# Moving four PSUM casts from VectorE to ScalarE, and the bank of TensorE's filler matmuls

## The chip, the cores and the metric

The kernel runs on 1 core of a Trainium2 chip. The metric is the device time of one execution in microseconds (us). In what follows PE is TensorE (matmuls), ACT is ScalarE, DVE is VectorE, POOL is GpSimd and SP is SyncE, as in the profile; PSUM is the accumulator memory that TensorE writes, here 8 banks of 512 fp32 columns, and only ScalarE and VectorE read it in this kernel.

## The reference

A sigmoid attention over 8 batches of 12 heads, 448 positions and 64 features, followed by a gated MLP over the 3584 tokens:

```python
scores = (q @ k.T) / sqrt(64) - log(448)      # per batch and head, 448 x 448
x = sigmoid(scores) @ v                       # the attention output
x = x.transpose(0, 2, 1, 3).reshape(3584, 768)
h = x @ w_in                                  # 768 -> 2048
g = h * sigmoid(beta * h)
out = g @ w_out                               # 2048 -> 768
```

## The kernel before, in words

All matmuls take fp16 operands and accumulate in fp32. The work is cut into tasks, each of a few instructions of one engine. The 96 (batch, head) pairs form 24 **groups** of four heads; a group g has two "slots", 2g and 2g+1, of two heads each, and a batch has three groups. For each group:

- `sG.j` (`visit`, L229) or, for the first batch, `hG.half.k` (`half_visit`, L249): the scores of a block of keys, by matmuls of 32 rows (L969, several at a time in parts of the array) into pairs of PSUM banks, one pair for each slot or tile.
- `eG.j.i` (`weigh`, L222 and L978): ScalarE reads such a pair and writes sigmoid(scale * score + bias) to SBUF as fp16 (L979). One instruction reads 896 columns; a few read 448.
- `aG.half.i` (`attend`, L279): the product with v, matmuls of L991, one bank for each slot.
- `xS.half` (L308): the bank is cast to fp16 into `xT` by `put_x` (L1000), 448 columns for each slot, or 224 in the first batch, where the queries are taken in two halves.

The MLP's first product of a batch (`d`, and `p`, an arrangement with fewer multiplications) runs on `xT`, with a sigmoid on ScalarE (L1024) and a product on VectorE (L1033); the second product (`tP.i.part`, L1009 and L1011) takes two tiles of 128 tokens at a time, in seven products, and its `o` tasks copy and add banks into `osb` (L1152 is the copy on ScalarE, `oP.1`).

**The order.** TensorE's order of tasks and the order of the loads on POOL's queue are written out by hand (`PE_ORDER`, L768, and `LOAD_ORDER`, L804). The function `plan` (L614) goes through them with estimated durations, when the program is built, and fixes from that the banks, the buffers and the order of the tasks on ScalarE and VectorE: each of these takes the ready task that has been ready longest. The order that the plan gives is emitted with a manual schedule; on the chip each engine runs its instructions strictly in that order, and semaphores make it wait for what it needs. The waits are set for each bank: an instruction that writes a bank waits for whoever read the bank before.

**Fillers.** Between 5 and 36 us of the plan, where TensorE is planned to wait, `plan` puts matmuls of zeros there (L740): `fills` (L595) gives them a free bank if there is one, and otherwise writes only the unused 64 columns (448 to 511) of the bank of the first filler task (`work.idle_bank`), which is bank 0. They are emitted by `idle` (L871, matmul in L873), right before the task that waits.

**The places that the change touches.** In the plan of the kernel before the following are met:

- TensorE's order has `h1.1.1`, then 18 filler matmuls of 64 columns in bank 0, then `a0.1.0`, then four fillers in bank 7, then `h2.1.1`. The task `h1.1.0` ahead of them wrote the bank pairs (6, 7) and (0, 1), which ScalarE's `eh1.1.0.0` and `eh1.1.0.1` read in this order; `h1.1.1` wrote the pairs (2, 3) and (4, 5), which `eh1.1.1.0` and `eh1.1.1.1` read. `a0.1.0` writes bank 6, and `h2.1.1` writes the pairs (0, 1) and (6, 7).
- For groups 6 and 7 (both of batch 2) TensorE's order has `a6.0.0`, `s7.0`, then products of tile pair 1, with `s8.0` after eight of them; and `a7.0.0`, `s8.2`, three products of tile pair 2, `s8.3`. `s8.1`, `s8.2` and `s8.3` all use the bank pairs (0, 1) and (6, 7), in this order. `s8.3` has 16 matmuls in two passes: the first four of a pass write the pair (0, 1), the next four (6, 7). The casts of group 6 are `x12` and `x13`, those of group 7 are `x14` and `x15`. ScalarE's order is `e7.1.1`, `e7.0.0`, `e7.0.1`, `o1.1` and later `e8.1.1`, `e8.2.0`, `e8.2.1`, `o2.1`, `e8.3.0`.

Of the kernel before, what the change touches and what calls it, by code (L numbers as in the profile page):

```python
# [15 lines left out]
B, H, S, D = 8, 12, 448, 64  # L16
# [9 lines left out]
NPAIR = H // 2  # L26
# [9 lines left out]
QH = S // 2  # L36
# [13 lines left out]
def mm(n):  # L50
    return max(n / 2400 + 0.0025, 0.057)
# [4 lines left out]
WARM = 36.0  # L56
SHORT = 0.03
START_END, START_RATE = 7.3, 115.0
# [16 lines left out]
def dve_us(n):  # L75
    return 0.076 + 1.04e-3 * n, 0.24 + 1.04e-3 * n
# [15 lines left out]

WHOLE = tuple(range(16))
SPLIT = (6, 7)
ENGINES = ("PE", "ACT", "DVE", "POOL", "SP", "Z")
FREE_AT = {"PE": 1.0, "ACT": 3.3, "DVE": 0.9, "POOL": 1.2, "SP": 0.7, "Z": 0.0}
MODES = {"s": 0, "s64": 1, "v": 2, "v64": 3, "d": 4}
# [13 lines left out]
class Work:  # L111
# [167 lines left out]
    def attend(self, g, c0=0, n=S, parts=((0, 1),)):  # L279
        k, b = self.k, g // QPB  # L280
        for part in parts:
            slots = [2 * g + x for x in part]
            ats = {(s, jt): self.at[s, jt, c0] for s in slots for jt in range(JF + 1)}
            us = JF * len(slots) * mm(n) + SWITCH + mm(n)
            first = b not in self.x_first
            name = f"a{g}.{c0 // QH}.{part[0]}"
            if c0 == 0 and n == QH and part == (0,):
                vs = self.v_low[b]
            else:
                vs = self.v_ready[b]  # L290
            pe = self.pe_task(name, us, [w for w, _ in ats.values()] + vs, mode="v", end_mode="v64", take=["xT"] if first else [], banks="S" * len(slots), good=n == S)
            if first:
                self.x_first[b] = pe
            for w in {id(w): w for w, _ in ats.values()}.values():
                self.users.setdefault(w.i, [w, 0])
            order = [(s, i, jt) for i, s in enumerate(slots) for jt in range(JF)] + [(s, i, JF) for i, s in enumerate(slots)]
            pe.emit = lambda t, order=order, ats=ats: k.values(
                [(s, t.bank[i], jt, ats[s, jt][0].slot["attn"], ats[s, jt][1]) for s, i, jt in order], self.v_first[b].slot["v"], n
            )
            for w in {id(w): w for w, _ in ats.values()}.values():  # L300
                last = self.last_user.get(w.i)
                if last is not None:
                    last.give.remove((w, "attn"))
                    pe.after.append(last)
                pe.give.append((w, "attn"))
                self.last_user[w.i] = pe
            for i, s in enumerate(slots):
                c = self.add("DVE", f"x{s}.{c0 // QH}", dve_us(n), [pe], give_banks=[(pe, i)])  # L308
                c.emit = lambda t, i=i, s=s, pe=pe: k.put_x(self.x_first[b].slot["xT"], s % NPAIR, c0, n, pe.bank[i])
                self.x_ready[b, c0].append(c)  # L310
                self.x_by[b, s % NPAIR, c0] = c
            self.av[g, c0, part[-1]] = pe
        if c0 + n == S:
            if g % QPB == QPB - 1:
                pe.give.append((self.v_first[b], "v"))
# [204 lines left out]
    def build(self):  # L520
# [39 lines left out]
        for c0 in (0, QH):  # L560
            for dc in range(NDC):
                if dc not in WHOLE:
                    firsts.append(self.plain(0, dc, c0, QH))
                elif c0:
                    firsts += self.split(dc) if dc in SPLIT else [self.plain(0, dc, 0, S)]
        free = self.add("Z", "xfree0", (0.0, 0.02), firsts, give=[(self.x_first[0], "xT")])
# [28 lines left out]
def fills(us, banks, first):  # L595

    if us < 0.12:
        return None
    if not banks:
        return [(first[0], S, FREE_COLS, int(us / SHORT))]  # L600
    long = int(us / mm(512))
    short = int((us - long * mm(512)) / mm(128))
    return [(banks[0], 0, n, c) for n, c in ((512, long), (128, short)) if c]
# [10 lines left out]
def plan(work, pe_names, load_names):  # L614
# [6 lines left out]
    bank_free, bank_busy, good = [0.0] * 8, [False] * 8, [False] * 8  # L621
    users = [[] for _ in work.tasks]
    left = [len(t.deps) for t in work.tasks]
    ready_at = [0.0] * len(work.tasks)
    ready = {e: [] for e in ENGINES}
    split_columns(queue["PE"])
# [6 lines left out]
    free, events, n = dict(FREE_AT), [], 0  # L633
    pe_end = FREE_AT["PE"]
# [41 lines left out]
    def can(t):  # L676
        return all(slot(r) is not None for r in t.take) and (not t.banks or find(t.banks) is not None)

    def begin(t, now):
        for r in t.take:  # L680
            i = t.slot[r] = slot(r)
            busy[r][i] = True
        extra = 0.0
        if t.banks:
            got, mend = find(t.banks)
            for x in got:
                bank_busy[x] = True
                good[x] = t.good
            t.bank = got[::2] if t.banks[0] == "D" else got
            t.mend = mend if t.banks[0] == "F" else []  # L690
            extra = 0.19 if any(t.mend) else 0.0
        t.start = now
        order.append(t)
        return extra

    now = 0.0
    while events:
        now = events[0][0]
        batch = []
        while events and events[0][0] <= now + 1e-9:  # L700
            batch.append(heapq.heappop(events))
        for _, kind, _, x in batch:
            if kind:
                for u in users[x.i]:
                    left[u.i] -= 1
                    if left[u.i] == 0:
                        ready_at[u.i] = now
                        ready[u.eng].append(u)
                for t, r in x.give:
                    i = t.slot[r]  # L710
                    busy[r][i], slots[r][i] = False, now
                for t, i in x.give_banks:
                    for y in (t.bank[i], t.bank[i] + 1) if t.banks[0] == "D" else (t.bank[i],):
                        bank_busy[y], bank_free[y] = False, now
        for e in ENGINES:
            if free[e] > now + 1e-9:
                continue
            if e in queue:
                if at[e] >= len(queue[e]):
                    continue  # L720
                t = queue[e][at[e]]
                if left[t.i] or not can(t):
                    continue
                if e == "POOL":
                    if at[e] >= 8 and lands[at[e] - 8] > now:
                        heapq.heappush(events, (lands[at[e] - 8], 0, n, e))
                        n += 1
                        continue
                    begin(t, now)
                    at[e] += 1  # L730
                    free[e] = now + t.occ
                    kb, rate = t.kb
                    dma_free = service(max(dma_free, now + 1.83), kb, rate)
                    late = 4.3 if now > 55 else 2.7 if now > 12 else 0.3 if dma_free < 6.3 else 1.2 if dma_free < 11 else 1.8
                    lands.append(dma_free + min(late, 2.0))
                    done = dma_free + late
                else:
                    wait = now - pe_end
                    rest = [x for x in range(8) if not bank_busy[x] and bank_free[x] <= pe_end]
                    t.fill = fills((wait - 0.15) / (2 if now < START_END else 1), rest, work.idle_bank.bank) if 5 < now < WARM else None  # L740
                    extra = begin(t, now)
                    at[e] += 1
                    if mode is not None and t.form != mode:
                        extra += SWITCH
                    mode = t.form if t.mode == "d" else t.end_mode
                    pe_end = free[e] = now + extra + t.occ
                    done = now + extra + t.lat
            else:
                cand = [t for t in ready[e] if can(t)]
                if not cand:  # L750
                    continue
                t = min(cand, key=lambda t: (ready_at[t.i] - t.soon, t.i))
                ready[e].remove(t)
                begin(t, now)
                free[e] = now + t.occ
                done = now + t.lat
                if t.kb:
                    dma_free = max(dma_free, now + 1.0) + t.kb[0] / t.kb[1]
            heapq.heappush(events, (free[e], 0, n, e))
            t.done = done  # L760
            heapq.heappush(events, (done, 1, n + 1, t))
            n += 2
# [51 lines left out]
class Emitter:  # L814
# [182 lines left out]
                    tile_position=(base, hh * D),  # L997
                )

    def put_x(self, x, p, c0, n, bank):  # L1000
        self.nc.vector.tensor_copy(out=self.xT[x][:, p, c0 : c0 + n], in_=self.bank(bank, n))  # L1001

# [234 lines left out]
```

## Time and profile before

| what | value |
|---|---|
| time, median of 3 runs | 372.1 us (371.88 to 372.85) |
| time of the profiled execution | 372.93 us |
| its span (first to last instruction) | 370.6 us |
| PE busy | 364.2 us, 98% of the span |
| DVE busy | 278.1 us, 75% |
| ACT busy | 250.5 us, 68% |
| data moved by DMA | 34.81 MB |

The profiled execution is one run under the hardware profiler. Its own time is 2.3 us longer than its span, the time around the instructions. In a row of the timeline stand the start, the duration, engine, line, operation, output and input with the shapes, the count of instructions merged into the row, and in brackets how long the engine had been idle and whom it waited for. Matmuls overlap: the profiler's end of one lies a little after the start of the next.

### The profile page before, as it was taken

The page shows a single profiled execution, that of the slowest core. Times are in us where ns is not written, and L with a number is a line of the kernel's source. Part 1 is how long each engine was busy: PE and PEld are TensorE (multiplying, and loading weights), DVE is VectorE, ACT ScalarE, POOL GpSimd, SP SyncE. Part 2 cuts the span into 40 slices and gives each one's busy share as a digit, 9 for nine tenths or more (in the row PEclk, how much of TensorE's full clock was granted, in tenths as well). Part 3 has the DMA queues.
Part 4 walks back from the last instruction along what each step waited for, and adds up shares of the span by engine and source line. Part 5 has one row for each costly group of instructions (what it writes and reads, how often), then busy time and mean ns, then how long its engine had stood idle before and what let it go on. Part 6 is the DMA issues. An engine that isn't in the chain of part 4 may idle for free.

```text
span 370.6 us, 10079 instructions
## 1 busy us (share of the span) xinstructions
PE 364.2 (98%) x4182; PEld 229.2 (62%) x4182; DVE 278.1 (75%) x577; ACT 250.5 (68%) x407; POOL 67.0 (18%) x113
## 2 busy tenths in 40 slices
PE   8989999999999999999999999999999999999996
PEld 4644445744556954479544794489544894579664
DVE  3436889999666988678787698689686686777865
ACT  5879975676467776768777689778756787546400
POOL 7837143500006301040004300070000000000000
PEclk9999999999999999999999999999999999999999
DMA  8999999932137942593016930095021300120124
GB/s 164 194 201 195 204 204 201 200 41 54 33 88 96 231 58 38 123 135 83 3 27 126 202 68 0 3 153 109 0 56 33 88 2 3 33 55 0 45 84 128
DMA packets 42845, 34.81 MB, mean 94 GB/s; under 512 B 21920, under 2 KB 39344, under 8 KB 42800
## 3 DMA queue, kind: packets, MB, share of 16 engines
q0 software_dynamic: 36688, 22.47, 43.6%
q1 hardware_dynamic: 5968, 11.65, 11.4%
q8 instruction: 32, 0.52, 0.6%
q14 instruction: 13, 0.11, 0.1%
q10 hardware_dynamic: 144, 0.07, 0.1%
HBM read 45.62 MB, written 11.01 MB: 153 GB/s over the span
## 4 chain that ended last, share of the span: by engine, by line
PE 92%; DVE 4%; DMA 2%; ACT 1%; issue 1%; POOL 0%; POOLq 0%
PE ps L1011 49%; PE ps L1009 20%; PE ps L969 11%; PE ps L991 10%; DMA raw<-in_k_dram 2%; DVE gt L1033 2%; PE ps L873 2%; DVE ps L1033 1%; DVE kT L956 1%; ACT sg L1024 0%; ACT attn L979 0%; POOL raw L893 0%; DVE xT L1001 0%; ACT ps L1088 0%; DVE sum L1033 0%
## 5 line engine op out<-in xcount | busy, mean ns | idle before, releaser
L979 ACT ACTIVATE attn<-ps 128x896 f16<-128x896 f32 (+1 forms) x171 | 145.1, 904 | 56.0 <-PE ps L969 55.2
L1024 ACT ACTIVATE sg<-ps,beta_sb 128x448 f32<-128x448 f32 x128 | 76.4, 637 | 29.1 <-PE ps L1011 16.4
L1033 DVE TENSOR_TENSOR gt<-ps,sg 128x448 f16<-128x448 f32 x128 | 75.2, 614 | 7.2 <-ACT sg L1024 6.6
L1009 PEld LDWEIGHTS <-w_in 128*64 128x64 f16 x1308 | 64.2, 110 | 6.1 <-issue 1.8
L1011 PEld LDWEIGHTS <-sum 128*128 128x128 f16 x480 | 44.8, 98 | 35.1 <-issue 8.1
L1033 DVE TENSOR_TENSOR sum<-gt 128x1024 f16<-128x1024 f16 x70 | 46.8, 683 | 22.7 <-PE ps L1011 21.1
L1011 PEld LDWEIGHTS <-w_in 128*128 128x128 f16 x531 | 50.5, 98 | 17.7 <-issue 2.9
L1011 PE MATMUL ps<-xT,w_in 128*128 128x224 f16 (+1 forms) x327 | 54.1, 304 | 0.0
L969 PE MATMUL ps<-qT,kT 32*128 32x448 f16 (+3 forms) x864 | 50.7, 340 | 0.1
L1009 PE MATMUL ps<-xT,w_in 128*64 128x224 f16 (+1 forms) x636 | 48.5, 277 | 0.0
L1001 DVE CAST xT<-ps 128x448 f16<-128x448 f32 (+1 forms) x54 | 29.0, 566 | 25.0 <-PE ps L991 24.9
L1011 PE MATMUL ps<-w_T,sum 128*128 128x384 f16 (+1 forms) x256 | 45.7, 322 | 0.0
L1033 DVE TENSOR_TENSOR ps<-ps,S 128x224 f32<-128x224 f32 x90 | 34.2, 392 | 14.9 <-ACT ps L1088 7.4
L1009 PE MATMUL ps<-xs,w_in 128*64 128x224 f16 x672 | 45.0, 259 | 0.1
L991 PE MATMUL ps<-attn,v 128*64 128x448 f16 (+3 forms) x432 | 42.0, 338 | 0.0
L1033 DVE TENSOR_TENSOR osb<-ps,osb 128x384 f32<-128x384 f32 (+1 forms) x72 | 38.6, 542 | 4.4 <-PE ps L1011 2.3
L1011 PE MATMUL ps<-w_out,sum 128*128 128x384 f16 x224 | 40.9, 327 | 0.0
L1011 PE MATMUL ps<-w_out,gt 128*128 128x384 f16 x212 | 39.6, 327 | 0.3 <-DVE xT L1001 0.3
L913 POOL DMA_DIRECT2D v<-in_v_dram x32 | 20.1, 631 | 104.8 <-PE ps L991 88.7
L991 PEld LDWEIGHTS <-v 128*64 128x64 f16 (+1 forms) x432 | 20.7, 108 | 20.0 <-issue 11.9
L1011 PEld LDWEIGHTS <-gt 128*128 128x128 f16 x212 | 19.1, 98 | 19.0 <-issue 8.0
L969 PEld LDWEIGHTS <-kT 32*128 32x128 f16 (+1 forms) x864 | 13.4, 96 | 24.1 <-issue 22.6
(38 smaller groups left out, 242.0 us busy)
## 6 DMA issues: line engine op xcount, KB each, us to landing
out_dram<-osb SPq DMA_DIRECT2D x100, 96.0 KB, 1.9
raw<-in_k_dram POOLq DMA_DIRECT2D x23, 224.0 KB, 7.2
raw<-in_q_dram POOLq DMA_DIRECT2D x21, 224.0 KB, 7.1
v<-in_v_dram POOLq DMA_DIRECT2D x32, 144.0 KB, 6.4
w_in<-in_moe_w_in_dram POOLq DMA_DIRECT2D x8, 384.0 KB, 9.3
w_out<-in_moe_w_out_dram POOLq DMA_DIRECT2D x4, 768.0 KB, 14.2
v<-in_v_dram POOLq DMA_DIRECT2D x16, 48.0 KB, 6.4
out_dram<-osb SPq DMA_DIRECT2D x4, 192.0 KB, 2.1
```

The lines of the kernel that those rows point to most:

```text
L873: self.nc.tensor.matmul(self.ps[:, x, c0 : c0 + n], self.still[:, 0:P], self.still[:, 0:n], start=(c0 == 0), stop=True, skip_group_check=True,
L913: self.nc.gpsimd.dma_start(out=to, in_=rows[:, :, JF * i * D : JF * (i + 1) * D])
L956: self.nc.vector.transpose(out=to, in_=frm)
L969: self.nc.tensor.matmul(self.ps[base : base + nk, d + hh, u0 : u0 + n], self.kT[k][lo : lo + BLK, jt * P : jt * P + nk, e], self.qT[q][lo ...
L979: self.nc.scalar.activation(out=self.at[slot][:, :, 0:n], in_=self.ps[:, d : d + 2, 0:n], func=AF.Sigmoid, bias=NEG_LOG_S, scale=MSCALE,)
L991: self.nc.tensor.matmul(self.bank(x, n)[hh * D : (hh + 1) * D], self.vs[v][base : base + nk, 2 * (s % NPAIR) + hh, jt], self.at[at][base : ...
L1001: self.nc.vector.tensor_copy(out=self.xT[x][:, p, c0 : c0 + n], in_=self.bank(bank, n))
L1009: self.nc.tensor.matmul(out[lo : lo + D], w[:, lo : lo + D], x, tile_position=(0, lo), **kw)
L1011: self.nc.tensor.matmul(out, w, x, **kw)
L1024: self.nc.scalar.activation(out=self.sg[slot][:, 0:n], in_=self.bank(x, n), func=AF.Sigmoid, bias=0.0, scale=self.beta_sb[:, dc : dc + 1],)
L1033: self.nc.vector.tensor_tensor(out=out, in0=in0, in1=in1, op=getattr(ALU, op))
```

## The change

Three things change in the text of the program. A new constant `XA` names the groups 6 and 7; for these `attend` gives the four casts `x12` to `x15` to ScalarE, with `put_x` using ScalarE's copy, instead of VectorE. And `plan` keeps a set `read` of the banks that a planned reader is reading at the time, so that fillers without a free bank go to a bank outside this set whose reader has not begun.

```diff
+XA = (6, 7)
...
             for i, s in enumerate(slots):
-                c = self.add("DVE", f"x{s}.{c0 // QH}", dve_us(n), [pe], give_banks=[(pe, i)])
-                c.emit = lambda t, i=i, s=s, pe=pe: k.put_x(self.x_first[b].slot["xT"], s % NPAIR, c0, n, pe.bank[i])
+                on_act = g in XA
+                c = self.add("ACT" if on_act else "DVE", f"x{s}.{c0 // QH}", (copy_us if on_act else dve_us)(n), [pe], give_banks=[(pe, i)])
+                c.emit = lambda t, i=i, s=s, pe=pe: k.put_x(self.x_first[b].slot["xT"], s % NPAIR, c0, n, pe.bank[i], on_act)
...
+    read = set()
+
     def begin(t, now):
...
+        for o, i in t.give_banks:
+            read.update((o.bank[i], o.bank[i] + (o.banks[0] == "D")))
...
                 for t, i in x.give_banks:
+                    read -= {t.bank[i], t.bank[i] + (t.banks[0] == "D")}
...
-                    t.fill = fills((wait - 0.15) / (2 if now < START_END else 1), rest, work.idle_bank.bank) if 5 < now < WARM else None
+                    beside = [x for x in work.idle_bank.bank + list(range(7, -1, -1)) if x not in read and (bank_busy[x] or bank_free[x] <= pe_end)]
+                    t.fill = fills((wait - 0.15) / (2 if now < START_END else 1), rest, beside or work.idle_bank.bank) if 5 < now < WARM else None
...
-    def put_x(self, x, p, c0, n, bank):
-        self.nc.vector.tensor_copy(out=self.xT[x][:, p, c0 : c0 + n], in_=self.bank(bank, n))
+    def put_x(self, x, p, c0, n, bank, on_act):
+        copy = self.nc.scalar.copy if on_act else self.nc.vector.tensor_copy
+        copy(out=self.xT[x][:, p, c0 : c0 + n], in_=self.bank(bank, n))
```

In the program that comes out, nothing else moves. TensorE runs the same matmuls in the same order, with the same banks but for one run of fillers: the 18 ahead of `a0.1.0` now write columns 448 to 511 of bank 5 instead of bank 0. The first of them no longer has a wait; `a0.1.0`'s first matmul and `h2.1.1`'s first matmul, which had none, now each have a wait for ScalarE, and so has `eh1.1.1.1`, which reads bank 5, for the fillers. Three other runs of 64-column fillers that stood in bank 0 stay there. On ScalarE `x12` and `x13` stand between `e7.1.1` and `e7.0.0`, and `x14` and `x15` between `e8.1.1` and `e8.2.0`; VectorE's order is the old one without these four. The queues of POOL and SP, all loads and all stores are the same.

## The prediction

> **What bounds the kernel now.** I read the page first: its busy shares, and the chain of work that ended last by engine.
>
> ```profile
> span 370.6 us, 10079 instructions
> PE 364.2 (98%) x4182; PEld 229.2 (62%) x4182; DVE 278.1 (75%) x577; ACT 250.5 (68%) x407; POOL 67.0 (18%) x113
> PE 92%; DVE 4%; DMA 2%; ACT 1%; issue 1%; POOL 0%; POOLq 0%
> ```
>
> PE is busy for 364.2 of 370.6 us and makes up 92% of the chain. So a microsecond counts only where PE stands still, or is made to. Next come the waits of PE over the whole span (us in total, times, longest).
>
> ```profile
> PE ps L873 <- ACT attn L979: 1.4, 1, 1.4
> PE ps L873 <- DVE dummy L866: 1.2, 1, 1.2
> PE ps L1011 <- DVE xT L1001: 0.3, 1, 0.3
> PE ps L873 <- issue: 0.2, 1, 0.2
> ```
>
> PE's waits come to 3.1 us. The second is the start of the kernel. The largest is a filler (L873) that waits for a weighing of ScalarE (L979): matmuls that do no work hold up TensorE. The timeline of PE shows where, that of ACT whom it waits for, and the chain of waits the last piece.
>
> ```profile
> 19.73 1.10 PE L969 MATMUL ps<-qT,kT 32*128 32x224 f16 x32
> 22.18 0.69 PE L873 MATMUL ps<-sum 128*128 128x64 f16 x18 [1.35 <-ACT attn L979]
> 22.79 0.69 PE L991 MATMUL ps<-attn,v 128*64 128x224 f16 x8
> 23.41 0.72 PE L873 MATMUL ps<-sum 128*128 128x512 f16 x4
> 24.06 0.70 PE L969 MATMUL ps<-qT,kT 32*128 32x224 f16 x16
> ...
> 20.40 0.92 ACT L979 ACTIVATE attn<-ps 128x896 f16<-128x896 f32 x1 [0.36 <-PE ps L969]
> 20.40 2.97 ACT L979 ACTIVATE attn<-ps 128x896 f16<-128x896 f32 x4 [0.36 <-PE ps L969]
> 24.82 0.92 ACT L979 ACTIVATE attn<-ps 128x896 f16<-128x896 f32 x1 [1.45 <-PE ps L969]
> ...
> 21.21 0.92 ACT attn L979
> 22.13 0.04 issue
> 22.18 0.69 PE ps L873 x18
> ```
>
> The first row is `h1.1.0` and `h1.1.1`, over at 20.83 (19.73 + 1.10). The 18 fillers should fill the wait after it. Instead the first of them waits until 22.13, the end of the second of ScalarE's four weighings: `eh1.1.0.1`, which reads banks 0 and 1. The fillers write bank 0. `a0.1.0`, at 22.79, writes bank 6, and bank 6 is read by the first weighing, over at 21.32 (20.40 + 0.92). So `a0.1.0` runs 1.47 us after its bank is free, behind a wait that isn't its own and the 0.61 us of the fillers (22.79 - 22.18).
>
> **The change, part one: the fillers in bank 5.** Bank 5 belongs to `eh1.1.1.1`, the fourth weighing; it doesn't begin before 22.8, while 18 fillers that start after `h1.1.1` are long over. So the fillers begin at once. Matmuls overlap by 0.07 (22.18 + 0.69 = 22.87, and the next row begins at 22.79), so they begin at about 20.76 and leave PE free at 20.76 + 0.61 = 21.37. `a0.1.0` also needs the first weighing: 21.32, and 0.05 for the semaphore (22.13 to 22.18). That gives 21.37 too. I take 21.38 for the start of `a0.1.0`, against 22.79: **1.41 us earlier**. Bounds: 1.47 if the wait costs nothing, and 0.61 if `a0.1.0` had to wait for the second weighing itself.
>
> What is late next? `h2.1.1` follows after `a0.1.0` and four fillers, at 24.06 - 1.41 = 22.65. Its banks 0 and 1 are free at 22.13; bank 6 needs the cast of `a0.1.0`, which moves with it. Its output goes to ScalarE, which begins at 24.82 today after 1.45 us of idleness, so ScalarE can take it up to 1.45 us earlier: 1.41 fits, by 0.04. The two are this close because ScalarE's four weighings do not move.
>
> Then the loads: the DMA queues are full in this stretch, and their data won't land earlier. The nearest load is k of group 3, transposed by VectorE after the cast of `a0.1.0`.
>
> ```profile
> 23.59 0.39 DVE L1001 CAST xT<-ps 128x224 f16<-128x224 f32 x1 [3.96 <-PE ps L991]
> 23.90 0.57 DVE L956 STREAM_TRANSPOSE kT<-raw 128x384 f32<-128x384 f32 x1
> ...
> 13.28 0.57 POOL L893 DMA_DIRECT2D raw<-in_k_dram  x1
> raw<-in_k_dram POOLq DMA_DIRECT2D x1, 224.0 KB, 8.7
> ...
> DVE xT L1001 <- PE ps L991: 8.4, 8, 4.0
> DVE gt L1033 <- ACT sg L1024: 3.5, 3, 1.8
> ...
> POOL v L913 <- PE ps L991: 88.7, 4, 40.9
> ```
>
> It is issued at 13.28 and lands 8.7 later, at 21.98; the transpose moves from 23.90 to 22.49 and still finds it. The next two rows are all the waits of VectorE between 22.5 and 76 us: none is for a DMA. So the loads have slack everywhere there. Later POOL's queue itself waits for buffers, most of all for PE, as the last row shows for the whole span; such loads move with PE. After 22.18 PE waits once more, for 0.3 us, on a cast of its own product; that moves along. So I carry the 1.41 us to the end.
>
> **Part two: the casts of group 7.** The copy on ScalarE is bounded by its own rows; the last three are a copy, a copy and a weighing in direct sequence.
>
> ```profile
> L1152 ACT COPY osb<-ps 128x384 f32<-128x384 f32 x14 | 6.8, 484 | 17.3 <-PE ps L1011 17.3
> L907 ACT CAST raw<-osb 128x448 f16<-128x448 f32 x1 | 0.6, 566 | 0.1
> L869 ACT ACT_TABLE_LOAD x1 | 1.3, 1283 | 1.2 <-PEq L1223 1.2
> ...
> 116.71 0.34 ACT L1085 COPY S<-ps 128x224 f32<-128x224 f32 x1
> 116.94 0.36 ACT L1088 COPY ps<-ps 128x224 f32<-128x224 f32 x1
> 117.22 0.93 ACT L979 ACTIVATE attn<-ps 128x896 f16<-128x896 f32 x1
> ```
>
> From 384 columns in 0.484 and 224 in 0.35 I get 0.84 ns a column ((0.484 - 0.35) / 160), and 0.54 us for 448. What counts is the interval to the next instruction: 0.23 from copy to copy and 0.28 from copy to weighing at 224 columns. With 0.19 for 224 more columns (224 x 0.84 ns): 0.42 and 0.47, so 0.89 for the pair. Bounds: 0.51 (no price for columns) and 1.13 (2 x 0.566, no overlap).
>
> [...]
>
> ```profile
> 103.66 1.16 DVE L1001 CAST xT<-ps 128x448 f16<-128x448 f32 x2 [0.28 <-PE ps L991]
> 106.75 0.65 DVE L942 STREAM_TRANSPOSE qT<-raw 128x448 f32<-128x448 f32 x1 [1.94 <-PE ps L969]
> ...
> 104.22 1.73 ACT L979 ACTIVATE attn<-ps 128x896 f16<-128x896 f32 x2 [1.65 <-PE ps L969]
> ...
> 106.11 0.40 PE L969 MATMUL ps<-qT,kT 32*64 32x448 f16 x8
> 106.11 0.60 PE L969 MATMUL ps<-qT,kT 32*64 32x448 f16 x16
> ```
>
> On VectorE the two casts run from 103.66 to 104.82, and then it is idle for 1.94: taking them away frees nobody. On ScalarE they begin at about 103.68, and `e8.2.0`, today at 104.22, begins at 103.68 + 0.89 = 104.57: 0.35 later. Its second part `e8.2.1` ends at 105.95 today (104.22 + 1.73), and at 106.30 then. The next scores, `s8.3` at 106.11, write banks 0 and 1 first, and with the fifth matmul bank 6, which `e8.2.1` frees. The row of eight is what had begun by 106.14: matmuls of different parts of the array start within hundredths of a microsecond of each other, so the fifth starts at 106.12 today; it will have to wait for 106.30 + 0.05 = 106.35. PE is held up by **0.23 us**, the matmul stream behind `s8.3` with it. Bounds: with 0.51 for the pair nothing is late (104.19), 0 us; with 1.13 it is 0.24 more, 0.47. Behind the casts on ScalarE `o2.1` waits too, 0.35 later; its reader on PE is only the fourth task after `s8.3`. I take 0.23.
>
> **Part three: the casts of group 6.** The same two copies, at 91.28.
>
> ```profile
> 91.28 0.62 DVE L1001 CAST xT<-ps 128x448 f16<-128x448 f32 x1
> 91.82 1.73 ACT L979 ACTIVATE attn<-ps 128x896 f16<-128x896 f32 x2 [1.06 <-PE ps L969]
> 93.43 0.49 ACT L1152 COPY osb<-ps 128x384 f32<-128x384 f32 x1
> 97.57 0.92 ACT L979 ACTIVATE attn<-ps 128x896 f16<-128x896 f32 x1 [3.65 <-PE ps L969]
> ```
>
> `e7.0.0` moves from 91.82 to 92.17, and `o1.1` ends at 94.27 instead of 93.92. The next user of their banks comes with the scores just before 97.57, and ScalarE is idle for 3.65 before that: this cover hides all of it. Without it the price would be the same 0.35. VectorE's transposes behind `x12` get 0.5 us earlier, which no one waits for. Cost 0.
>
> **The sum.** -1.41 + 0.23 + 0 = **-1.18 us**. The profiled execution took 372.93 (span 370.6 and 2.3 around it) and would take 371.75. It lies at the top of the runs shown; against their median of 372.1 the forecast is 370.9.
>
> **The rivals.**
>
> (A) *The wait stays.* If `a0.1.0` itself had to wait until 22.18 (a semaphore that counts up to the second weighing instead of the first), only the fillers' 0.61 would be hidden: -0.61 + 0.23 = -0.38, 371.7. For it: 21.32 and 22.13 are neighbours on one engine, counted by one semaphore. Against it: `h2.1.1`'s first matmul, which writes bank 0, has a wait of its own for ScalarE now, which would not be needed if `a0.1.0` had waited that far.
>
> (B) *The gain is caught on the way.* ScalarE is nearly full after 22 us: it can follow by only 1.45, and a load that lands just in time would stop the rest. Lost as a whole, with the 0.23 left, that is 372.1 + 0.23 = 372.3; lost by half, 371.6. Against it: the waits of PE and VectorE above, in which no DMA occurs.
>
> (C) *Slower: the copies bring table loads.* If a plain copy between sigmoids made ScalarE load its table for the copy and again for the sigmoid, at 1.283 us each, `e8.2.0` would come 2.57 us later still; at `s8.3` this stands on PE in full, 2.57 + 0.23, and with the 1.41 the time is 1.39 longer: 373.5. (At group 6 the 2.57 + 0.35 = 2.92 would just fit into the 3.65.) It decides from 1.18 us more on ScalarE at group 7. Against it: the 14 copies of L1152 and those of L1085 and L1088 stand between sigmoids already, and the trace has one table load in all. [...]
>
> **How the numbers follow.** My forecast has 0.74: gains between 0.9 and 1.5 us (0.47 to 0 for the copies against 1.41 to 1.47), so 370.6 to 371.2, and a few tenths to either side since the runs of before alone differ by 1.0 us. (A) has 0.10, (B) 0.10, (C) 0.06. The range 370.2 to 372.0 holds the forecast, (A) and the edge of (B). About 0.3%, 1.1 us, can be told from no change. The forecast's 1.18 lies near this line: of its 0.74 I put 0.62 beyond it, 0.12 within. With (A) and (B) that makes 0.62 faster, 0.32 the same, 0.06 slower.
>
> **What would show it.** In the profile after: the L873 row of 18 fillers at about 20.8, with no wait; PE's largest wait then is the start. `a0.1.0` (L991, x8) at 21.4, `h2.1.1` at 22.65, ACT's idle before its next weighing at most 0.1. All later rows 1.4 earlier up to 104; the row of 16 matmuls of `s8.3` about 0.2 longer than 0.60, and from there on rows 1.2 earlier. A start of `a0.1.0` at 22.2 would be (A); a shift that shrinks between 24 and 80 us (B); more than one ACT_TABLE_LOAD (C).

## The result and the profile after

| | before | after |
|---|---|---|
| median of 20 runs | 372.43 us (371.88 to 375.72) | 371.05 us (370.60 to 372.02) |
| profiled execution | 372.93 us, span 370.6 | 371.16 us, span 369.4 |
| wait of PE ahead of `a0.1.0` | 1.35 us | none |
| start of `a0.1.0` | 22.79 | 21.41 |
| from `a7.0.0` to the product after `s8.3` | 4.64 us | 4.82 us |

The ratio is 0.9956 (0.9942 to 0.9970): the change makes the kernel 0.44% faster (0.30 to 0.58). Ratios here and below leave out executions that took over 1.5% longer than the fastest of the same kernel, which are two of e8_no_fillers; medians include them. The span falls by 1.2 us; the sum of the prediction was -1.18. In the changed kernel's text the lines stand 9 or 10 further down: L873 is L882 there, L969 is L978, L979 is L988, L991 is L1000, L1001 is L1011, L1011 is L1021 and L1152 is L1162.

The page of the changed kernel, its busy shares and its chain by engine:

```profile
span 369.4 us, 10082 instructions
PE 364.1 (99%) x4182; PEld 229.2 (62%) x4182; DVE 275.9 (75%) x573; ACT 252.2 (68%) x411; POOL 66.9 (18%) x113
PE 93%; DVE 4%; DMA 2%; ACT 1%; issue 0%; POOL 0%; POOLq 0%
```

PE's busy time is the same to 0.1 us; the span shrinks because PE stands still for less. The four casts show as 2.2 us that DVE no longer has and 1.7 us that ACT has in addition. The waits of PE in the same kernel (us in total, times, longest):

```profile
PE ps L882 <- DVE dummy L875: 1.2, 1, 1.2
PE ps L882 <- issue: 0.4, 1, 0.4
PE ps L1021 <- DVE xT L1011: 0.3, 1, 0.3
```

A fourth, of 0.2 us, is a wait of `h` scores for a transposed k (L965) at 8.28, ahead of the places changed. The filler's wait for ACT, the largest before, is missing; the start of the kernel is now the largest. A stall by "issue" has grown from 0.2 to 0.4 us; it is dealt with at the end. PE's timeline around the place, again of the changed kernel:

```profile
19.75 1.09 PE L978 MATMUL ps<-qT,kT 32*128 32x224 f16 x32
20.78 0.70 PE L882 MATMUL ps<-sum 128*128 128x64 f16 x18
21.41 0.69 PE L1000 MATMUL ps<-attn,v 128*64 128x224 f16 x8
22.03 0.72 PE L882 MATMUL ps<-sum 128*128 128x512 f16 x4
22.68 0.70 PE L978 MATMUL ps<-qT,kT 32*128 32x224 f16 x16
```

The 18 fillers begin 0.06 before the profiled end of `h1.1.1` (19.75 + 1.09), in the usual overlap, and `a0.1.0` follows at 21.41. The same stretch on ACT and DVE, whether each can follow:

```profile
20.43 0.92 ACT L988 ACTIVATE attn<-ps 128x896 f16<-128x896 f32 x1 [0.36 <-PE ps L978]
20.43 4.36 ACT L988 ACTIVATE attn<-ps 128x896 f16<-128x896 f32 x6 [0.36 <-PE ps L978]
25.22 0.92 ACT L988 ACTIVATE attn<-ps 128x896 f16<-128x896 f32 x1 [0.44 <-PE ps L978]
```

```profile
22.21 0.39 DVE L1011 CAST xT<-ps 128x224 f16<-128x224 f32 x1 [2.55 <-ACT attn L988]
22.52 0.57 DVE L965 STREAM_TRANSPOSE kT<-raw 128x384 f32<-128x384 f32 x1
```

ACT runs six weighings in one row where it had four and then 1.45 us of nothing; DVE transposes k of group 3 at 22.52, without a wait. Both take the whole 1.4 us.

At group 7 the distance that counts is from the start of `a7.0.0` to that of the product behind `s8.3`. In the kernel before these rows are:

```profile
102.00 1.61 PE L991 MATMUL ps<-attn,v 128*64 128x448 f16 x16
106.64 2.12 PE L1011 MATMUL ps<-w_out,sum 128*128 128x384 f16 x12
```

The distance is 4.64 us. In the changed kernel `a7.0.0` starts at 100.62. ACT and PE behind it:

```profile
102.27 0.97 ACT L1011 CAST xT<-ps 128x448 f16<-128x448 f32 x2 [1.08 <-PE ps L1000]
103.12 1.75 ACT L988 ACTIVATE attn<-ps 128x896 f16<-128x896 f32 x2
```

```profile
104.73 0.58 PE L978 MATMUL ps<-qT,kT 32*64 32x448 f16 x8
104.73 0.78 PE L978 MATMUL ps<-qT,kT 32*64 32x448 f16 x16
105.44 0.82 PE L1021 MATMUL ps<-w_out,sum 128*128 128x384 f16 x4
```

The product behind `s8.3` starts at 105.44, after 4.82 us. The copies take 0.85 us from the first to the weighing behind them. That weighing's second part ends at 103.12 + 1.75 = 104.87; the row of 16 matmuls is 0.18 longer than before (0.78 against 0.60), and the row of eight reaches into the stall (0.58 against 0.40). Against the same instructions of before, PE's rows stand at -1.38 us from `a0.1.0` to `s8.3`, and at -1.20 from there to the end.

### The profile page after: what moved, and what is told of

Same layout as the page of the kernel before. It is cut to its first block, busy times and chain, and to the rows that moved or that the text cites. A ratio compares the mean times of both kernels' runs of the same rounds, so it can differ in the third digit from the quotient of the medians.

```text
span 369.4 us, 10082 instructions
## 1 busy us (share of the span) xinstructions
PE 364.1 (99%) x4182; PEld 229.2 (62%) x4182; DVE 275.9 (75%) x573; ACT 252.2 (68%) x411; POOL 66.9 (18%) x113
## 4 chain that ended last, share of the span: by engine, by line
PE 93%; DVE 4%; DMA 2%; ACT 1%; issue 0%; POOL 0%; POOLq 0%
PE ps L1021 49%; PE ps L1019 20%; PE ps L978 12%; PE ps L1000 10%; DVE gt L1043 2%; DMA raw<-in_k_dram 2%; PE ps L882 2%; DVE ps L1043 1%; DVE kT L965 1%; ACT sg L1034 0%; POOL raw L902 0%; DVE xT L1011 0%; ACT ps L1098 0%; DVE sum L1043 0%; DVE osb L1043 0%
## 5 line engine op out<-in xcount | busy, mean ns | idle before, releaser
L988 ACT ACTIVATE attn<-ps 128x896 f16<-128x896 f32 (+1 forms) x171 | 145.2, 905 | 51.5 <-PE ps L978 50.5
L1021 PEld LDWEIGHTS <-sum 128*128 128x128 f16 x480 | 44.8, 98 | 35.1 <-issue 8.1
L1021 PEld LDWEIGHTS <-w_in 128*128 128x128 f16 x531 | 50.5, 98 | 17.7 <-issue 2.5
L1021 PE MATMUL ps<-xT,w_in 128*128 128x224 f16 (+1 forms) x327 | 54.1, 304 | 0.0
L978 PE MATMUL ps<-qT,kT 32*128 32x448 f16 (+3 forms) x864 | 50.8, 340 | 0.2 <-DVE kT L965 0.2
L1021 PE MATMUL ps<-w_T,sum 128*128 128x384 f16 (+1 forms) x256 | 45.7, 322 | 0.0
L1011 DVE CAST xT<-ps 128x448 f16<-128x448 f32 (+1 forms) x50 | 26.6, 562 | 23.4 <-PE ps L1000 20.8
L1000 PE MATMUL ps<-attn,v 128*64 128x448 f16 (+3 forms) x432 | 42.0, 339 | 0.0
L1021 PE MATMUL ps<-w_out,sum 128*128 128x384 f16 x224 | 40.9, 327 | 0.0
L1021 PE MATMUL ps<-w_out,gt 128*128 128x384 f16 x212 | 39.6, 327 | 0.3 <-DVE xT L1011 0.3
L1000 PEld LDWEIGHTS <-v 128*64 128x64 f16 (+1 forms) x432 | 20.7, 108 | 20.0 <-issue 11.9
L1021 PEld LDWEIGHTS <-gt 128*128 128x128 f16 x212 | 19.1, 98 | 19.0 <-issue 7.6
L978 PEld LDWEIGHTS <-kT 32*128 32x128 f16 (+1 forms) x864 | 13.5, 96 | 24.2 <-issue 22.3
```

The costliest lines, as they stand in the source:

```text
L978: self.nc.tensor.matmul(self.ps[base : base + nk, d + hh, u0 : u0 + n], self.kT[k][lo : lo + BLK, jt * P : jt * P + nk, e], self.qT[q][lo ...
L988: self.nc.scalar.activation(out=self.at[slot][:, :, 0:n], in_=self.ps[:, d : d + 2, 0:n], func=AF.Sigmoid, bias=NEG_LOG_S, scale=MSCALE,)
L1000: self.nc.tensor.matmul(self.bank(x, n)[hh * D : (hh + 1) * D], self.vs[v][base : base + nk, 2 * (s % NPAIR) + hh, jt], self.at[at][base : ...
L1021: self.nc.tensor.matmul(out, w, x, **kw)
```

## The experiments

**The theories.** Mine: the time falls by what one filler's wait cost, about 1.4 us less 0.2 for the copies at group 7; bank 5 matters only because nobody is reading it yet. One rival: the casts help, alone or together with the fillers. Another: what is saved at one place of the kernel is lost again at a later one. The medians of three batches stand against runs of the kernel before on the same chip: 372.39 for e1, e2, e3 and e5, 372.2 for e4, e6, e7 and e8, 372.91 for r1, r2 and e9.

| run | median us | ratio to before (95%) | `h1.1.0` to `a0.1.0`, us | `a7.0.0` to the product after `s8.3`, us |
|---|---|---|---|---|
| before | | | 3.06 | 4.64 |
| changed kernel | 371.05 | 0.9956 (0.9942 to 0.9970) | 1.66 | 4.82 |
| e1_fillers_only | 371.34 | 0.9977 (0.9959 to 0.9995) | 1.66 | 4.64 |
| e2_casts_only | 372.54 | 1.0004 (0.9995 to 1.0012) | 3.07 | 4.82 |
| e3_no_18 | 370.92 | 0.9962 (0.9951 to 0.9973) | 1.64 | 4.64 |
| e4_cast6_only | 371.04 | 0.9974 (0.9960 to 0.9988) | 1.72 | 4.64 |
| e5_no_38 | 370.13 | 0.9944 (0.9929 to 0.9959) | 1.66 | 4.64 |
| e6_twice | 372.42 | 1.0003 (0.9992 to 1.0015) | 1.66 | 5.95 |
| e7_bank7 | 371.75 | 0.9983 (0.9965 to 1.0001) | 2.26 | 4.64 |
| e8_no_fillers | 377.03 | 1.0090 (1.0063 to 1.0117) | 2.00 | 4.64 |
| r1_after | 371.03 | 0.9949 (0.9926 to 0.9972) | 1.66 | 4.82 |
| r2_fillers_only | 371.14 | 0.9949 (0.9929 to 0.9968) | 1.66 | 4.64 |
| e9_no_56 | 370.14 | 0.9914 (0.9885 to 0.9943) | 1.64 | 4.64 |

The two last columns are distances between starts on PE. They are free of what happens elsewhere in a run, and agree to some hundredths from run to run.

### The two halves

e1_fillers_only leaves the casts on DVE:

```diff
-XA = (6, 7)
+XA = ()
```

> The changed kernel with XA empty: the 18 fillers in bank 5, all casts on VectorE as before. My theory: the whole gain is the filler's wait for the second weighing (1.38 us in the trace after), and the casts cost 0.18 at s8.3. So the span is 370.6 - 1.4 = 369.2, shorter than that of the changed kernel by 0.2, and s8.3 shows no stall between its fourth and fifth matmul. Rival (the casts help, by relieving VectorE): the span is longer than 369.4.

e2_casts_only leaves the fillers in bank 0:

```diff
-fills((wait - 0.15) / (2 if now < START_END else 1), rest, beside or work.idle_bank.bank)
+fills((wait - 0.15) / (2 if now < START_END else 1), rest, work.idle_bank.bank)
```

> The changed kernel with the 18 fillers back in bank 0, the four casts on ScalarE. My theory: the filler waits again until 22.1, PE's largest wait is 1.35 again, and the casts cost 0.2: span 370.8, time within 0.1% of before. Rival (the casts help): span under 370.6, by part of the 1.2 that the change gave.

With the casts alone the old wait of PE is back, and the row of `s8.3` has the 0.78 of the changed kernel. PE's timeline of e2_casts_only:

```profile
22.43 0.69 PE L882 MATMUL ps<-sum 128*128 128x64 f16 x18 [1.35 <-ACT attn L988]
...
106.37 0.78 PE L978 MATMUL ps<-qT,kT 32*64 32x448 f16 x16
```

Its time is that of before (1.0004). So the rival that the casts help falls: no part of the gain is the casts'. With the fillers alone both distances are the good ones, 1.66 and 4.64, and the 0.18 us at `s8.3` is shown to be the price of the casts. Yet its time, 371.34, isn't below that of the changed kernel, as I had expected, and its span, 370.2 us, lies where I had put the rival (over 369.4). The distances rule that rival out all the same; the time is lost elsewhere. The trace of e1_fillers_only shows two stalls of PE by "issue" that are longer than those of the changed kernel, or not there in it:

```profile
14.93 0.25 PE L882 MATMUL ps<-sum 128*128 128x64 f16 x3 [0.79 <-issue]
...
124.14 0.64 PE L1019 MATMUL ps<-xs,w_in 128*64 128x224 f16 x9 [0.47 <-issue]
```

### One group's casts

e4_cast6_only keeps the fillers in bank 5 and moves only `x12` and `x13`:

```diff
-XA = (6, 7)
+XA = (6,)
```

> The changed kernel with XA = (6,): the casts of group 6 on ScalarE, those of group 7 on VectorE. My theory: group 6's casts cost nothing, since ScalarE is idle for more than 3 us behind them, and all of the 0.18 is group 7's. From the start of a6.0.0 to that of s8.0 and from that of a7.0.0 to that of t2.2.1 PE takes 7.36 and 4.64, as before (4.82 after). Rival (each cast costs its share): half of the 0.18 shows up between a6.0.0 and s8.0.

The casts on ACT and the next weighing that follows a pause, in e4_cast6_only:

```profile
90.00 0.97 ACT L1011 CAST xT<-ps 128x448 f16<-128x448 f32 x2 [0.49 <-PE ps L1000]
...
96.31 0.92 ACT L988 ACTIVATE attn<-ps 128x896 f16<-128x896 f32 x1 [3.35 <-PE ps L978]
```

ACT's idle time before that weighing falls from 3.65 to 3.35 us and hides the copies; from `a6.0.0` to `s8.0` PE takes 7.36 us in every kernel of the table. Group 6 costs nothing. At group 7 the distance is 4.64: the 0.18 us belongs to `x14` and `x15` alone.

### The price of a copy, doubled

e6_twice is the changed kernel, with the two casts of group 7 executed twice (the second time with the same result):

```diff
-c.emit = lambda t, i=i, s=s, pe=pe: k.put_x(..., on_act)
+c.emit = lambda t, i=i, s=s, pe=pe, on_act=on_act: [k.put_x(..., on_act) for _ in range(2 if g == 7 else 1)]
```

> The changed kernel with each of the two casts of group 7 done twice on ScalarE (the second writes the same data again, and waits for the first to be written: about 0.6 more each). My theory: ScalarE's slack there is used up by the first pair, so the added 1.2 us stands on PE at s8.3 in full: a7.0.0 to t2.2.1 takes 4.64 + 0.18 + 1.2 = 6.0, and nothing of it is given back; span 370.6, the gain of the fillers eaten up. Rival (later work absorbs it): PE loses under 0.6.

ACT and PE in e6_twice:

```profile
102.23 2.10 ACT L1011 CAST xT<-ps 128x448 f16<-128x448 f32 x4 [1.08 <-PE ps L1000]
104.22 1.73 ACT L988 ACTIVATE attn<-ps 128x896 f16<-128x896 f32 x2
```

```profile
105.20 0.39 PE L978 MATMUL ps<-qT,kT 32*64 32x448 f16 x4 [0.44 <-ACT attn L988]
106.01 0.59 PE L978 MATMUL ps<-qT,kT 32*64 32x448 f16 x12 [0.42 <-ACT attn L988]
```

The second pair takes 104.22 - 102.23 - 0.85 = 1.14 us, and PE is later by 5.95 - 4.82 = 1.13: with the slack used up, ACT's time stands on PE in full, first at bank 0 and then at bank 6. The whole gain is gone (1.0003). This is the mechanism of rival (C) of the prediction, with copies in the place of table loads: 1.14 us more on ACT at this place cancel the change.

### Which bank, and whether fillers at all

e3_no_18 is the kernel before without the 18 fillers ahead of `a0.1.0`; all others stay where they were, and the casts too:

```diff
-if 5 < now < WARM else None
+if 5 < now < WARM and t.name != "a0.1.0" else None
```

> The kernel before without the 18 fillers ahead of a0.1.0 (zero matmuls, no part of the output); casts on VectorE. My theory: what counts is that nothing ahead of a0.1.0 waits for bank 0's reader; a0.1.0 then waits for bank 6's reader alone and starts at 21.4, and the span is 369.2, as with fillers in bank 5, although PE stands idle for 0.55. Rival (the fillers keep PE fast and are needed): matmuls after the gap are slower, or the span is over 369.5.

e7_bank7 has the casts on DVE and the 18 fillers in bank 7, which the first of the four weighings reads:

```diff
-rest, beside or work.idle_bank.bank)
+rest, [7] if t.name == "a0.1.0" else beside or work.idle_bank.bank)
```

> XA empty, and the 18 fillers in bank 7, which the first weighing (eh1.1.0.0) reads, not the second. My theory: a filler waits for the reader of the bank that it writes; so the first filler waits for the end of the first weighing, 0.81 before that of the second, and a0.1.0 follows after 0.62 of fillers. From the start of h1.1.0 to that of a0.1.0: 3.06 before, 1.66 with bank 5, and 2.25 here; span about 369.8. Rival (what matters is only that it isn't the bank that is read last, or any bank of a planned reader costs the same): 1.66, or 3.06.

PE's timeline of e3_no_18, then that of e7_bank7:

```profile
19.47 1.10 PE L969 MATMUL ps<-qT,kT 32*128 32x224 f16 x32
21.11 0.69 PE L991 MATMUL ps<-attn,v 128*64 128x224 f16 x8 [0.55 <-ACT attn L979]
```

```profile
19.98 1.10 PE L978 MATMUL ps<-qT,kT 32*128 32x224 f16 x32
21.62 0.69 PE L882 MATMUL ps<-sum 128*128 128x64 f16 x18 [0.54 <-ACT attn L988]
22.24 0.69 PE L1000 MATMUL ps<-attn,v 128*64 128x224 f16 x8
```

Without these fillers `a0.1.0` waits 0.55 us for its own bank and starts as early (1.64); the time is that of the changed kernel (0.9962). So the gain is a wait taken away, and bank 5 brings nothing that leaving the fillers out doesn't. In bank 7 the fillers wait for the first weighing, and `a0.1.0` starts 0.62 later than it could (2.26, where 2.25 was expected). The three banks order themselves by how long a weighing that has begun still holds them: bank 0, held by the second weighing, gives 3.06; bank 7, held by the first, 2.26; bank 5, whose weighing hasn't begun, 1.66. The times say less: 0.9983 (0.9965 to 1.0001) for bank 7 can't be told from no change, and its span, 370.4, is longer than the 369.8 expected. No filler writes a column that the reader of its bank reads; still it waits for the whole reader: 1.35 us in bank 0, 0.54 in bank 7.

### Fewer fillers

e5_no_38 is e1_fillers_only without the 38 fillers ahead of `a0.0.0`:

```diff
-if 5 < now < WARM else None
+if 5 < now < WARM and t.name != "a0.0.0" else None
```

> XA empty, 18 fillers in bank 5, and no fillers ahead of a0.0.0 (38 zero matmuls from 13.1 to 14.9, no part of the output). My theory, from the same reading: a0.0.0 needs bank 2 from ScalarE (13.27) and the load of v (13.11), so its fillers hold it up from 13.35 to 14.90; without them a0.0.0 starts at 13.35. What is late next is h0.1.0, whose q half lands at 14.4 and is transposed by 14.9: it starts at about 14.95 instead of 16.15. So 1.2 us more: span 368.0. Rival (ScalarE or the loads are the bound from 15 us on): ScalarE has weighings until 15.5, and the gain is 0.6 or less; or PE gets slow, and there is none.

In e5_no_38 PE starts `a0.0.0` at 13.48, where 14.88 stood before:

```profile
13.48 1.50 PE L1000 MATMUL ps<-attn,v 128*64 128x224 f16 x16 [0.19 <-ACT attn L988]
14.91 0.76 PE L978 MATMUL ps<-qT,kT 32*128 32x224 f16 x16
...
20.36 0.69 PE L1000 MATMUL ps<-attn,v 128*64 128x224 f16 x8
```

The 38 fillers were as wrong as the 18, for another reason: they ran longer than the wait that they fill. `a0.1.0` gains another 1.05 us, where 1.2 was expected. The time is 370.13 (0.9944), but the span of the profiled execution, 369.1, misses the 368.0 expected: PE's rows lose 0.61 us again at 251.5, where a stall "issue" of 0.41 stands, and 0.36 around 353.

e8_no_fillers leaves out all fillers, 145 matmuls:

```diff
-t.fill = fills(...) if 5 < now < WARM else None
+t.fill = None
```

> XA empty and no fillers at all but the first task of the kernel (they are zero matmuls, no part of the output); PE idles where they stood. My theory: fillers only cost where they hold up the task behind them, ahead of a0.0.0 and a0.1.0; PE's gaps without them are under 1.5 us each and leave its clock. Then a0.0.0 and a0.1.0 start as without the 38 fillers, at about 13.4 and 20.3, the matmuls of h1.0.0, h2.0.0 and h1.1.0 last as long as before, and the span is 368.2. Rival (fillers keep the clock up): the matmuls between 8 and 20 us get longer, the granted clock shows less than 9 tenths in the first slices, and the span is over 369.

My theory had this kernel among the fastest, with a span of 368.2; the ratio has it 0.9% slower, and the profiled execution, with a span of 372.0, 1.4 us longer than before. PE's groups by shape between 14 and 24 us in e8_no_fillers (busy time, mean ns of one), and the same from 14 to 22 us in the kernel before:

```profile
L1000 PE MATMUL ps<-attn,v 128*64 128x224 f16 x35 | 4.6, 392 | 0.1
L978 PE MATMUL ps<-qT,kT 32*128 32x224 f16 x52 | 3.5, 378 | 0.0
```

```profile
L991 PE MATMUL ps<-attn,v 128*64 128x224 f16 x30 | 2.4, 266 | 0.0
L969 PE MATMUL ps<-qT,kT 32*128 32x224 f16 x48 | 1.7, 259 | 0.0
```

The same matmuls take 1.46 to 1.47 times as long, and they did so earlier: between 6 and 14 us those of L978 take 373 ns on average, against 264 before. PE's timeline of e8_no_fillers, 16 matmuls in each row:

```profile
17.55 2.12 PE L1000 MATMUL ps<-attn,v 128*64 128x224 f16 x16
...
25.75 1.31 PE L1000 MATMUL ps<-attn,v 128*64 128x224 f16 x16
```

From about 25 us on they have the usual 1.31. So the fillers do keep PE's matmuls fast until then; my theory, in which they do nothing but fill waits, was wrong there. `a0.1.0` starts at 23.63 here, 2.9 us after e9_no_56 below. The executions of e8_no_fillers range from 372.25 to 378.06 us; the ten from 375 us up have a mean granted clock of 0.964 to 0.973, while in the profiled one, of 373.78 us, it is 1.00. The fastest, 372.25 us, has 0.982. The profiled execution is 0.4% above the median of before, 372.2; its slow matmuls don't account for the rest of the 0.9%, and what brings the clock down in the others stays open.

e9_no_56 keeps the fillers, but for the 38 and the 18 (the casts stay on DVE):

```diff
-if 5 < now < WARM else None
+if 5 < now < WARM and t.name not in ("a0.0.0", "a0.1.0") else None
```

> As the kernel without the 38 fillers ahead of a0.0.0, and without the 18 ahead of a0.1.0 either; the other fillers stay. My theory: both runs of fillers only hold up the task behind them, and the fillers that are left (27 and 50 of 64 columns, and the wide ones) keep PE fast; a0.0.0 at 13.4 and a0.1.0 at 20.3, span 368.3 to 368.6, the fastest of all. Rival (PE gets slow as in the kernel without fillers): matmuls of h0.1.0 and h1.1.0 take over 1.5 times as long, span over 369.5.

PE's timeline of e9_no_56:

```profile
13.86 1.31 PE L1000 MATMUL ps<-attn,v 128*64 128x224 f16 x16 [0.18 <-ACT attn L988]
15.11 0.95 PE L978 MATMUL ps<-qT,kT 32*128 32x224 f16 x16
...
20.72 0.69 PE L1000 MATMUL ps<-attn,v 128*64 128x224 f16 x8 [0.55 <-ACT attn L988]
```

The matmuls of `a0.0.0` have the usual 1.31 us, and so have those of the row after it: the row is long (0.95, against 0.58 before) because its fifth matmul waits to 15.44 for a weighing on ACT, while its matmuls last 260 ns on average, as before. So the fillers that are left keep PE's matmuls as fast as all of them did. The median is 370.14, beside 371.03 for the changed kernel in the same batch. Its ratio to before, 0.9914 (0.9885 to 0.9943), overlaps a little with that of r1_after, 0.9949 (0.9926 to 0.9972). Every execution of it, though, was shorter than every one of r1_after (369.64 to 370.40 against 370.81 to 372.46). With e5_no_38, at 370.13 in another batch, it has the lowest median here.

### Again: the changed kernel and its fillers alone

r1_after is the changed kernel, r2_fillers_only is e1_fillers_only, both unaltered, in one batch.

> The changed kernel once more, on the same chip as the next two. By my theory PE takes 344.0 from the start of a0.1.0 to that of t13.6.1 (343.84 in all kernels without a copy on ScalarE at group 7, where PE is not held up by its own instruction stream), and the time is 0.2 above that of the next kernel.

> Fillers in bank 5, casts on VectorE, once more. Its first run had PE held up twice where nothing but its own instruction stream is missing (0.79 ahead of a0.0.0, 0.47 at p2.2.3), each about 1.5 us after a fetch of instructions ended. If such stalls vary from execution to execution, the trace now has others, or none at p2.2.3, and the time is 0.2 under that of the changed kernel. Rival (the stalls belong to this program): the same stall at p2.2.3 again, and a time above that of the changed kernel.

Both come to 0.9949, so the 0.18 us of the casts, though seen in every trace, isn't seen in the time. From the start of `a0.1.0` to that of `t13.6.1` PE takes 344.02 us in r1_after, as expected (344.02 in the changed kernel and in e2_casts_only too; 343.84 in before, e3_no_18 and e4_cast6_only). In r2_fillers_only it takes 344.30, and in e1_fillers_only 344.56, where 343.84 would stand if nothing else held PE up. The waits of PE in r2_fillers_only show what eats it:

```profile
PE ps L882 <- issue: 0.4, 1, 0.4
PE ps L1019 <- issue: 0.2, 1, 0.2
```

The second stands in the first products of a later batch, at the same instruction as the 0.47 of e1_fillers_only, and is missing there in all other runs. Around it PE's rows lose 0.47 us, more than the stall alone. So the expectation that the time would be 0.2 under that of the changed kernel failed, and the rival by which a saving is lost later is right for this program: what it saves at 105 us it loses at 124. Casts on DVE alone don't bring that stall: e7_bank7, with casts on DVE and all the fillers, hasn't got it. Why this program has it stays open; the last section says what is known.

## Why the prediction was right

- **Fillers in bank 5.** Forecast: fillers at 20.76, `a0.1.0` at 21.38, 1.41 us earlier. Measured: 20.78, 21.41, 1.38. The clock times agree partly by luck, since what comes before varies: in r1_after `a0.1.0` starts at 21.05. The distance from `h1.1.0`, which doesn't vary so, fell from 3.06 to 1.66, by 1.40. That the wait of the fillers, and not the bank they went to, was the cause is shown by e3_no_18 and e7_bank7.
- **What is late next.** `h2.1.1` was forecast at 22.65 and began at 22.68; the transpose of k at 22.49 and 22.52. The DMA engines are full there, as said: from 9 to 74 us every slice of the DMA row in the page of before has 9 tenths or more, at 194 to 204 GB/s. ACT took the shift whole, as forecast with 0.04 us to spare. So rival (B) doesn't hold for the changed kernel: its shift stays at -1.38 from 21 to 104 us.
- **Casts of group 7.** The pair was forecast at 0.89 us and took 0.85; one copy is busy for 0.536 us (estimate: 0.54). The stall at `s8.3` was forecast at 0.23 and is 0.18. Mechanism and place were right: the fifth matmul waits for the end of `e8.2.1` at 104.87 and starts at 104.92, 0.18 us after the fourth, against under 0.01 in before. e6_twice shows it at a larger size.
- **Casts of group 6.** Forecast 0, measured 0, hidden by ACT's idle time as said.
- **Rival (A)**, that `a0.1.0` itself would wait to 22.18, falls by its start at 21.41. **Rival (C)** falls by the one row of table loads in the changed kernel, of its groups on ACT:

```profile
L1011 ACT CAST xT<-ps 128x448 f16<-128x448 f32 x4 | 1.9, 536 | 1.6 <-PE ps L1000 1.6
L878 ACT ACT_TABLE_LOAD x1 | 1.3, 1283 | 1.2 <-PEq L1233 1.2
```

- **The time.** Forecast 370.9, measured 371.05, which is 1.38 us below the median of before in the same batch. The sum was 1.18. The 370.9 started from a median of three runs, 372.1; from the 372.43 of twenty runs it would have been 371.25, so 0.20 too high where 370.9 was 0.15 too low: by the medians the fall is 0.2 larger than the sum. The sum and the fall of the span agree to 0.02 us, which is luck too: 0.03 too much gain at the fillers and 0.05 too much cost at the copies nearly cancel.
- **What it missed.** It held the step "matmuls that do no work hold up TensorE" for a matter of one wait. e5_no_38 and e9_no_56 show a second place, ahead of `a0.0.0`, where fillers cost another 1.05 us; and e8_no_fillers shows that without any of them PE's matmuls are slow until about 24.5 us, so that as a whole they are worth having (the ratio without them is 1.0090, part of it at a lower granted clock whose cause is open).

## What to carry to other kernels

Work that fills a wait must be shorter than it and must not wait longer itself (here 1.05 us for the 38 fillers, 1.40 for the 18): look at which bank it writes and who reads that bank, even if nobody reads those columns. When work moves to another engine, read at each place how much slack the bound engine's next use of that engine's output has: the same two copies cost 0 at group 6 and 0.18 us at group 7, and 1.13 where the slack was used up. Before removing filler matmuls as useless, measure the duration of the real ones beside them without fillers. Here 56 of the 145 could go, and not all.

## What the runs showed of the hardware

**PE stands still now and then, until 1.4 to 1.6 us after a fetch of instructions.** The stalls "issue" come shortly after packets of the queue that the profile calls "instruction". Its row in the page of before, and its row in the DMA view of e1_fillers_only from 121 to 124 us:

```profile
q8 instruction: 32, 0.52, 0.6%
```

```profile
q8 instruction: 1, 0.02, 1.9%
```

There are 32 packets of 16 KB, and PE has 8386 instructions in the trace (weight loads, matmuls and 22 others), 262 for each packet if all are PE's. Counted in all traces, its stalls "issue" lie at instruction 450, 2498, 2754 or 5826, whole multiples of 256 apart (2048, 256 and 3072); no run shows why. Those of the following runs end 1.4 to 1.6 us after a fetch is over: for the 36th of the 38 fillers ahead of `a0.0.0` the fetch ends at 13.12 and PE goes on at 14.63 in before; 13.33 and 14.93 in e1_fillers_only; 12.85 and 14.38 in r2_fillers_only. In the products at 124 us the fetch ends at 122.72 in e1_fillers_only and PE goes on at 124.14; where the fetch was over 1.7 us or more before that instruction was due, as in before (122.38, due at 124.53), after (121.50, due at 123.32) and r1_after (121.24), there is no stall. Fillers start 34 ns apart (35 in 1.19 us), the matmuls of `a0.0.0` behind them 78 (16 in 1.24), so among fillers PE goes through its instructions faster. The stalls that the profile lists measured 0.15 to 0.79 us and differ from run to run of one program. Why the fetch came later in the two runs with the fillers alone (122.72 and 122.00, against 121.50 and 121.24 in after and r1_after) stays open. With some 32 fetches in an execution, two such stalls at most are listed (e1_fillers_only, r2_fillers_only), and none in r1_after.

**PE's matmuls are slow for long without fillers, and the clock column doesn't show it.** The stretches view of e8_no_fillers from 16 to 26 us (us, then busy time and count of PE, PEld, DVE, ACT and POOL, then the granted clock, DMA share and GB/s):

```profile
16.00:26.00 10.00, 9.59 (x126) 4.75 (x122) 3.96 (x10) 6.63 (x11) 3.45 (x7) 1.00 1.40 199
```

PE is busy for 9.59 of 10 us, the granted clock reads 1.00, and until 24 us its matmuls of L1000 take 392 ns in the place of 266. It is their duration that has to be read.

The slow ones went on to about 24.5 us, after 10 us in which PE's timeline lists no wait (14.63 to 24.5), and L1000 takes 1.47 times as long as before. With fillers earlier on the same matmuls are fast: 266 ns in before, and 1.31 us for a row of 16 in e9_no_56, against 2.12 here. As the granted clock reads 1.00, no run here shows why fillers have this effect.

**Casts from PSUM are no slower on ACT than on DVE here.** One of 448 columns takes 536 ns on ACT and 0.43 us from one to the next, where the rows of before on DVE have 0.62 us for one and 1.16 for two, which is 0.54 from one to the next.
